# Layer 2 of a two-layer MoE: each group's outs issued inside the next group's first chain, quarters taken from PSUM

## The chip, the cores and the metric

The kernel runs on 1 core of one Trainium2 chip. The metric is the device time of one execution in microseconds (us); three runs of the kernel before gave a median of 1530.74 us (1524.88 to 1533.66). Lower is better.

## The reference

A linear attention (8 batches, 8 heads, 576 positions, width 64, normalised per position) gives 4608 tokens of width 512. They go through two feed-forward layers:

```
kv  = einsum('bhsd,bhse->bhde', k, v);  out = einsum('bhsd,bhde->bhse', q, kv)
x   = out / rms(out) * g_norm                        # 4608 x 512
h   = x @ w_in;  x2 = (h * cos(h)) @ w_out           # layer 1: 512 -> 2048 -> 512
y   = (((x2 @ w1) * (x2 @ w2)) @ w3) @ w_out2        # layer 2: 512 -> 1024 -> 1024 -> 512
```

Everything is float32.

## The kernel before

TensorE multiplies values of a rounded format (fp32r). An operand is held as a rounded half (hi, a copy by ScalarE) and a remainder (lo, a subtraction by VectorE or GpSimd); `split` (L120) issues the two. A product then takes three matmuls, hi·hi, hi·lo, lo·hi, under the lines L878, L879 and L880 for 512 columns, or a loop at L1275 for 384.

The attention and layer 1 take the first 854 us and are untouched. What follows is one program order written out by hand: each engine carries out its instructions in the order in which the code issues them.

**The wc stage (854 to 905 us).** `w3 @ w_out2` is multiplied out once, as `wc`. It has 16 steps (`emit_wc`, L1201), two halves of 8, each step 12 matmuls of 512 columns with one block of w3. A block is split two steps ahead (`split_w3`, L1175) into one of two buffers (`g_home`, L96). In between stand other pieces: the first group's right operands from x2 (`xc_steps`, L1225) on VectorE, and the first left operands from w1 and w2 (`w12_steps`, L1131) on GpSimd, in pieces named in the table `when` of the main function. At the end of each half `split_wc` splits four blocks of wc out of PSUM.

**Layer 2 (905 us to the end, `second`, L1377).** There are 12 groups: six of 768 tokens with the first half of the columns of w1 and w2 (h = 0), then the same six backwards with the second half (h = 1). A group is four chains (`Chain`). A chain is one 128-column strip of x2 @ w1 or x2 @ w2 times a 2 x 2 block scheme with 7 products, P1 to P7, each of 6 matmuls of 384 columns; its four results are the quarters q0 to q3. P1 and P2 (`open1`) make Y, which gives q0; P6 goes into X (`open2`); P5 goes into V and P7 into X (`open3`), which gives q3; P4 (`close1`) gives q2 from X, P3 (`close2`) gives q1 from V. A chain's P4 and P3 run inside the next chain, after its P2 and P6. X (two banks, "h"), V (two, "pa"), Y ("acc0", "acc1") and the outs ("acc2", "acc3") are all eight banks of PSUM.

X is read between products into a row of SBUF (`held`, L1283, ScalarE): s1 after P1, s2 after P6, s3 after P7. So P7 can't begin before s2 is taken. `done` (L1315) forms a quarter: the w1 chain of a pair keeps it in SBUF (`a`); the w2 chain adds the held row (L1334, into the row), multiplies by `a` (L1335, row by row in SBUF, or L1332 from X), and splits the product from SBUF (ScalarE L122, VectorE L124) into `ab`. The rows are 512 wide ("row", 5 buffers).

The **outs** are ab @ wc: six blocks of 128 tokens, each with two halves of 6 matmuls of 512 columns (`o_half`, L1351). Half 0 uses the first chain pair, half 1 the second; half 1 of blocks 0 to 2 needs q0 and q2 of the last chain, of blocks 3 to 5 q3 and q1. In h = 0 an out is copied (ScalarE for even blocks, L1366; VectorE for odd) and stored as a partial sum; in h = 1 VectorE adds the partial sum that was loaded back (L1372) and the result is stored. All these DMAs, and the loads of x2 (`x2r`, L1231), are issued on SP's queue.

At the end of a group the code issues: half 0 of block 0, then P4 and P3 of the fourth chain, half 0 of block 1, half 1 of blocks 0 and 1, then blocks 2 to 5. Then comes P1 of the next group.

x2 is split into 7 right operands for each group but the seventh, which has the sixth's. Its pieces are hung on places of the group before: `(k, 2, "o1")` is after `open1` of chain 2 of group k. ScalarE makes the hi halves, GpSimd the sums and the lo halves. The left operands for h = 1 are made in the sixth and seventh group.

Of the kernel before, what the change touches and what calls it, by code (L numbers as in the profile page):

```python
# [8 lines left out]
F32R = mybir.dt.float32r  # L9
# [4 lines left out]
P = 128  # L14
# [14 lines left out]
def f32(ap):  # L29
    return ap.bitcast(F32)  # L30
# [3 lines left out]
def kernel(  # L34
# [1140 lines left out]
    def split_w3(step):  # L1175
        half, c = step
        t = g_home([P, 2, 4, P], F32R, f"w3hl_{half}_{c}")
        w3[half, c] = t
        return split(t.rearrange("p i j f -> p i (j f)"), w3raw.pop(step), vec)
# [21 lines left out]
    def emit_wc(half, c):  # L1201

        t, o = w3.pop((half, c)), wo2[c]
        for j in range(4):
# [58 lines left out]
    class Chain:  # L1263
# [37 lines left out]
        def open3(self):  # L1301
            self.v = self.bank(ps_a, "pa", "V")
            self.product(5, self.v, first=True)
            self.product(7, self.x)
            self.done(3, self.v, self.held(self.x, "s3"))

        def close1(self):
            self.product(4, self.x, last=True)
            self.done(2, self.x, None)

        def close2(self):
            self.product(3, self.v, last=True)
            self.done(1, self.v, self.s2)

        def done(self, q, ps, s):  # L1315
# [26 lines left out]
            split(ab[self.h, self.g, j][:, :, H * sh:H * sh + H], s, vec)  # L1342
# [34 lines left out]
    def second():  # L1377
# [16 lines left out]

        on((0, 0, "o1"), split_wc, 1, 1)
        on((0, 0, "o2"), split_wc, 1, 2)
        on((0, 0, "o2"), split_wc, 1, 3)
        for k in range(len(order) - 1):
            if order[k + 1][1] == order[k][1]:
                continue  # L1400
            at = [(k, 1, "o3"), (k, 2, "o1"), (k, 2, "o2"), (k, 3, "o1"), (k, 3, "o2"),
                  (k, 3, "o3"), (k, 3, "end")]
            if k == NG:
                at[:3] = (k, 2, "o1"), (k, 2, "o2"), (k, 2, "o3")
            stages(lambda g=order[k + 1][1]: xc_steps(g, pool), at)
# [3 lines left out]
        def begin(dp, i):  # L1409
# [4 lines left out]
            (0, 0): ((k, 2, "c1"), (k, 2, "o3"), (k, 3, "o1"), (k, 3, "o2"), (k, 3, "o3")),  # L1414
            (0, 1): ((k, 3, "end"), (k, "o", 0), (k, "o", 1), (k, "o", 2), (k, "o", 3)),
            (1, 0): ((k, "o", 4), (k, "o", 5), (k + 1, 0, "o1"), (k + 1, 0, "o2"), (k + 1, 0, "o3")),
            (1, 1): ((k + 1, 1, "o1"), (k + 1, 1, "c1"), (k + 1, 1, "o2"), (k + 1, 1, "c2"),
                     (k + 1, 1, "o3")),
        }
        for key, at in places.items():  # L1420
# [4 lines left out]
        n = 0  # L1425
        for k, (h, g) in enumerate(order):
            prev = None
            for at in range(4):
                c = Chain(h, g, *divmod(at, 2))
# [17 lines left out]
            o_half(h, g, 0, 0)  # L1447
            prev.close1()
            prev.close2()
            do(k, 3, "end")  # L1450
            o_half(h, g, 1, 0)
            for s in range(GT // P):
                if s > 1:
                    o_half(h, g, s, 0)
                o_half(h, g, s, 1)
                do(k, "o", s)
# [136 lines left out]
    if True:  # L1593
# [24 lines left out]
        with tc.manual_schedule(  # L1618
# [24 lines left out]
            for i, ks in enumerate(((0, 1, 2, 3, 3), (4, 5, 6, 7, 7), (8, 9, 10, 11, 13),  # L1643
                                    (12, 13, 14, 15, 15))):
                for k in ks:
                    when.setdefault(k, []).append(sets[i])
            when.setdefault(2, []).append(sets[2])
            when.setdefault(4, []).append(sets[3])
            for k in (5, 6, 7, 12, 13, 14):
                when.setdefault(k, []).append(x0)  # L1650
            for k, step in enumerate(wc_steps):
# [3 lines left out]
                if k + 2 < len(wc_steps):  # L1655
                    split_w3(wc_steps[k + 2])
# [4 lines left out]
            split_wc(1, 0)  # L1661
            second()
# [59 lines left out]
```

## Time and profile before

| what | value |
|---|---|
| median of 3 runs | 1530.74 us |
| the profiled execution's own time | 1533.62 us |
| its span in the trace | 1531.8 us |
| TensorE's mean granted clock in it | 0.988 |
| TensorE, matmuls | 1458.9 us, 95% |
| VectorE | 960.1 us, 63% |
| ScalarE | 696.1 us, 45% |
| GpSimd | 649.0 us, 42% |
| first P1 of the 12 groups | 905.15 us |
| last add of an out | 1527.66 us |

The share of busy time counts overlapping matmuls by their modelled ends, so it is no measure of what could be saved; the waits of one engine and the length of a stage are. The first matmul of P1 starts, for the 12 groups, at 905.15, 965.86, 1017.05, 1068.25, 1119.46, 1170.67, 1216.53, 1275.56, 1326.72, 1379.46, 1430.65 and 1481.81 us. Each group holds the same 240 matmuls, so the distances can be compared with each other.

### The profile page before, as it was taken

What the parts mean: (1) busy time and instruction counts of PE and PEld (TensorE: products, weight loads), DVE (VectorE), ACT (ScalarE), POOL (GpSimd) and SP (SyncE); (2) the same over time, 40 slices, a digit from 0 to 9 for tenths busy, and PEclk for the clock granted to TensorE, in tenths of its full rate; (3) what the DMA queues carried; (4) which work ended last, traced back from release to release, by engine and by line L of the source; (5) the groups of instructions that cost most, each with busy time, mean ns of one, the idle gap of its engine ahead of it and who ended that gap; (6) DMA issues with size and microseconds to landing.
All of it is one profiled execution on the core that took longest, in us unless ns stands there. A gap on an engine that the chain in (4) does not pass through costs nothing.

```text
span 1531.8 us, 21181 instructions
## 1 busy us (share of the span) xinstructions
PE 1458.9 (95%) x7632; PEld 1240.0 (81%) x7632; DVE 960.1 (63%) x1408; ACT 696.1 (45%) x1328; POOL 649.0 (42%) x504
## 2 busy tenths in 40 slices
PE   8999999999999999999999978998899979889988
PEld 6877777787778889888888767987898969778878
DVE  4797575574879667898888555444544354455444
ACT  4666565555556455555555443323332442233221
POOL 0174664575554622221224465325522672355230
PEclk8999999999999999999999989999999999999999
DMA  8366986797589989999999710221122123312321
GB/s 315 119 209 185 325 266 202 243 316 242 198 302 346 362 296 316 344 333 355 336 357 357 258 42 15 69 83 50 46 70 96 42 76 117 124 43 82 124 83 56
DMA packets 146506, 298.75 MB, mean 195 GB/s; under 512 B 16256, under 2 KB 54240, under 8 KB 146400
## 3 DMA queue, kind: packets, MB, share of 16 engines
q1 hardware_dynamic: 145696, 296.80, 56.3%
q8 instruction: 60, 0.98, 0.3%
q10 hardware_dynamic: 704, 0.59, 0.1%
q14 instruction: 46, 0.38, 0.1%
HBM read 184.92 MB, written 112.42 MB: 194 GB/s over the span
## 4 chain that ended last, share of the span: by engine, by line
PE 72%; DVE 15%; ACT 5%; issue 3%; DMA 2%; POOL 2%; SPq 1%; ACTq 0%; DVEq 0%; POOLq 0%
PE X L1052 13%; PE X L1275 8%; PE h L878 7%; PE h L879 7%; PE h L880 7%; PE V L1052 6%; DVE s L1335 4%; PE o L878 3%; PE Y L1052 3%; PE o L879 3%; PE o L880 3%; DVE ab L124 3%; PE V L1275 3%; PE Y L1275 2%; ACT ab L122 2%
## 5 line engine op out<-in xcount | busy, mean ns | idle before, releaser
L124 POOL TENSOR_TENSOR xc<-x2r,xc 128x768 fp32r<-128x768 f32 x70 | 134.1, 1934 | 267.3 <-ACT xc L122 249.7
L1275 PE MATMUL X<-xc,w 128*128 128x384 f32 x1152 | 221.9, 337 | 17.8 <-ACT s L1283 17.8
L878 PE MATMUL h<-x,w_in 128*128 128x512 f32 x576 | 234.2, 407 | 4.0 <-DVE u L1520 3.8
L879 PE MATMUL h<-x,w_in 128*128 128x512 f32 x576 | 224.8, 390 | 0.2 <-DVE x L124 0.2
L880 PE MATMUL h<-x,w_in 128*128 128x512 f32 x576 | 225.0, 391 | 0.0
L1275 PEld LDWEIGHTS X<-xc,w 128*128 128x128 f32 x1152 | 202.2, 188 | 23.6 <-ACT s L1283 21.6
L1052 PE MATMUL X<-g_hl,wl 128*128 128x512 f32 (+1 forms) x960 | 199.7, 368 | 0.0
L1052 PEld LDWEIGHTS X<-g_hl,wl 128*128 128x128 f32 x960 | 167.3, 189 | 30.2 <-DVE wl L124 0.2
L124 POOL TENSOR_TENSOR g_hl<-g_raw,g_hl 128x1024 fp32r<-128x1024 f32 x29 | 73.6, 2537 | 232.3 <-ACT g_hl L122 168.1
L124 DVE TENSOR_TENSOR g_hl<-g_raw,g_hl 128x1024 fp32r<-128x1024 f32 x97 | 140.3, 1473 | 39.9 <-ACT g_hl L122 39.8
L1546 DVE SCALAR_TENSOR_TENSOR u<-h,r 128x512 f32<-128x512 f32 x136 | 93.5, 688 | 109.7 <-ACT r L1545 89.6
L122 ACT ACTIVATE g_hl<-g_raw 128x1024 fp32r<-128x1024 f32 x126 | 130.4, 1057 | 52.3 <-DMA g_raw<-g 42.8
L1283 ACT ACTIVATE s<-X 128x384 f32<-128x384 f32 x144 | 68.9, 486 | 173.1 <-PE X L1275 173.0
L878 PE MATMUL o<-wchl,ab 128*128 128x512 f32 x288 | 117.5, 408 | 27.8 <-DVE part L1372 10.9
L1545 ACT ACTIVATE r<-h 128x512 int32<-128x512 f32 x136 | 81.3, 597 | 131.0 <-PE h L880 130.5
L878 PEld LDWEIGHTS h<-x,w_in 128*128 128x128 f32 x576 | 108.1, 188 | 35.8 <-DVE u L1520 9.1
L880 PEld LDWEIGHTS h<-x,w_in 128*128 128x128 f32 x576 | 108.1, 188 | 23.3
L879 PEld LDWEIGHTS h<-x,w_in 128*128 128x128 f32 x576 | 108.3, 188 | 22.9 <-DVE x L124 0.7
L880 PE MATMUL o<-wchl,ab 128*128 128x512 f32 x288 | 115.9, 403 | 3.5 <-DVE ab L124 3.5
L879 PE MATMUL o<-wchl,ab 128*128 128x512 f32 x288 | 114.9, 399 | 0.0
L122 ACT ACTIVATE ab<-s 128x384 fp32r<-128x384 f32 x72 | 37.8, 525 | 163.2 <-DVE s L1335 163.2
L1275 PE MATMUL V<-xc,w 128*128 128x384 f32 x576 | 109.6, 334 | 0.0
(164 smaller groups left out, 2608.0 us busy)
## 6 DMA issues: line engine op xcount, KB each, us to landing
g_raw<-g SPq DMA_DIRECT2D x126, 512.0 KB
x2r<-x_all SPq DMA_DIRECT2D x44, 384.0 KB
kvraw<-in_kv_main_dram SPq DMA_DIRECT2D x32, 512.0 KB
g<-ta SPq DMA_DIRECT2D x32, 512.0 KB
g<-tb SPq DMA_DIRECT2D x32, 512.0 KB
g<-u SPq DMA_DIRECT2D x28, 512.0 KB
g<-u SPq DMA_DIRECT2D x40, 256.0 KB
part<-o SPq DMA_DIRECT2D x36, 256.0 KB
```

The source lines that it names most:

```text
L122: hi = nc.scalar.activation(dst[:, 0], src, AF.Copy)
L124: lo = lo_engine.tensor_tensor(dst[:, 1], src, f32(dst[:, 0]), ALU.subtract)
L878: nc.tensor.matmul(ps, w[0], x[0], start=first, stop=False)
L879: nc.tensor.matmul(ps, w[0], x[1], start=False, stop=False)
L880: return nc.tensor.matmul(ps, w[1], x[0], start=False, stop=last).ins
L1052: nc.tensor.matmul(ps, w[:, a, i2, ws], g[:, b, q], start=first and half == 0 and q == 0 and n == 0, stop=last and final and q == KH - 1 a ...
L1275: nc.tensor.matmul(ps, w[:, self.i, a, k], x[:, b, k], start=first and k == 0 and n == 0, stop=last and k == 1 and n == 2, skip_group_chec ...
L1283: nc.scalar.activation(s, ps, AF.Copy)
L1335: vec.tensor_tensor(s, s, a, ALU.mult)
L1545: nc.scalar.activation(r, h_ps[n], AF.Identity, bias=0.25, scale=INV_2PI)
L1546: nc.vector.scalar_tensor_tensor(u, h_ps[n], INV_2PI, r, ALU.mult, ALU.subtract)
```

## The change

There are four parts.

1. **The outs' place** (`second`). A group's outs no longer stand behind its fourth chain but inside the first chain of the next group (`edge`): P1, P2, then P4 of the old chain, half 0 of blocks 0 and 1, P6, half 1 of block 0, P3 of the old chain, half 1 of block 1 and both of block 2, P5, P7, then blocks 3 to 5. Only the twelfth group's outs stand behind it.
2. **Values in PSUM** (`done`). The sum and the product of a quarter are written to PSUM (`to`: Y for q0 and q3, X for q2, V for q1), and the split reads them there. The first chain's Y lies in a "pa" bank.
3. **w3's blocks** lie in a ring of four buffers (two `g_home`, two pairs of rows), and are split three steps ahead instead of two.
4. **Places**: the pieces of x2's operands and of the w1, w2 sets hang on other places; five pieces of the last set of h = 0 go into the first group, and the split of wc's block (1, 0) stands after the first `open1`.

```
     def split_w3(step):
         half, c = step
-        t = g_home([P, 2, 4, P], F32R, f"w3hl_{half}_{c}")
+        if c % 4 < 2:
+            t = g_home([P, 2, TB], F32R, f"w3hl_{half}_{c}")
+            t = t[:, 0], t[:, 1]
+        else:
+            t = tuple(row(f"w3hl_{half}_{c}_{i}").bitcast(F32R) for i in range(2))
...
-            y = self.bank(ps_acc, f"acc{n % 2}", "Y")
-            self.product(2, y, first=True, last=True)
-            self.done(0, y, s)
+            self.y = self.bank(*((ps_acc, f"acc{n % 2}") if n else (ps_a, "pa")), "Y")
+            self.product(2, self.y, first=True, last=True)
+            self.done(0, self.y, s, self.y)
...
-            self.done(3, self.v, self.held(self.x, "s3"))
+            self.done(3, self.v, self.held(self.x, "s3"), self.y)
...
-            self.done(2, self.x, None)
+            self.done(2, self.x, None, self.x)
...
-            self.done(1, self.v, self.s2)
+            self.done(1, self.v, self.s2, self.v)
...
-            if s is None:
-                s = row(f"ab_{self.name}")[:, 0:H]
-                vec.tensor_tensor(s, ps, a, ALU.mult)
-            else:
-                vec.tensor_tensor(s, ps, s, ADD)
-                vec.tensor_tensor(s, s, a, ALU.mult)
+            if s is not None:
+                vec.tensor_tensor(to, ps, s, ADD)
+                ps = to
+            vec.tensor_tensor(to, ps, a, ALU.mult)
...
-            split(ab[self.h, self.g, j][:, :, H * sh:H * sh + H], s, vec)
+            split(ab[self.h, self.g, j][:, :, H * sh:H * sh + H], to, vec)
...
-            at = [(k, 1, "o3"), (k, 2, "o1"), (k, 2, "o2"), (k, 3, "o1"), (k, 3, "o2"),
-                  (k, 3, "o3"), (k, 3, "end")]
+            at = [(k, 1, "o3"), (k, 2, "o2"), (k, 2, "o3"), (k, 3, "o2"), (k, 3, "o3"),
+                  (k + 1, 0, "c1"), (k + 1, 0, "o2")]
...
+                edge = k > 0 and at == 0
                 c = Chain(h, g, *divmod(at, 2))
                 c.open1(n)
...
+                if edge:
+                    outs(k - 1, (0, 0), (1, 0))
                 c.open2()
                 do(k, at, "o2")
+                if edge:
+                    outs(k - 1, (0, 1))
                 if prev:
                     prev.close2()
                 do(k, at, "c2")
+                if edge:
+                    outs(k - 1, (1, 1), (2, 0), (2, 1))
                 c.open3()
                 do(k, at, "o3")
+                if edge:
+                    outs(k - 1, *both[6:])
...
-                if k + 2 < len(wc_steps):
-                    split_w3(wc_steps[k + 2])
+                if k + 3 < len(wc_steps):
+                    split_w3(wc_steps[k + 3])
...
-            split_wc(1, 0)
-            second()
+            second(sets[3])
```

The order of TensorE at the end of the fourth group and the start of the fifth, in the kernel before. A name's number tells one buffer's use from another; X_10080 and V_10134 are the fourth chain's, X_10279 the next group's first chain's, o_10160 and o_10190 the outs of blocks 0 and 1.

```order
L1275 MATMUL X_10080<-xc_5_9776,w_01_5_8644 128x384 x6
L878 MATMUL o_10160<-wchl_8551,ab_9961 128x512
...
L1275 MATMUL X_10080<-xc_6_9809,w_01_2_8605 128x384 x6
L1275 MATMUL V_10134<-xc_2_9779,w_01_6_8707 128x384 x6
L878 MATMUL o_10190<-wchl_8551,ab_9961 128x512
...
L878 MATMUL o_10160<-wchl_8557,ab_10098 128x512
...
L1275 MATMUL X_10279<-xc_0_10030,w_00_0_8381 128x384 x6
L1275 MATMUL Y_10288<-xc_1_10101,w_00_1_8384 128x384 x6
```

The same place after the change: X_10081 and V_10131 are the fourth chain's, X_10155 and Y_10164 the next group's.

```order
L1282 MATMUL X_10081<-xc_5_9806,w_01_5_8685 128x384 x6
L1282 MATMUL X_10155<-xc_0_10049,w_00_0_8386 128x384 x6
L1282 MATMUL Y_10164<-xc_1_10118,w_00_1_8389 128x384 x6
L1282 MATMUL X_10081<-xc_6_9834,w_01_2_8628 128x384 x6
L878 MATMUL o_10188<-wchl_8553,ab_9963 128x512
...
L878 MATMUL o_10195<-wchl_8553,ab_9963 128x512
...
L1282 MATMUL X_10155<-xc_4_10121,w_00_4_8467 128x384 x6
L878 MATMUL o_10188<-wchl_8559,ab_10099 128x512
...
L1282 MATMUL V_10131<-xc_2_9809,w_01_6_8742 128x384 x6
L878 MATMUL o_10195<-wchl_8559,ab_10099 128x512
```

P1 and P2 of the next group now stand ahead of the old chain's P4, and 12 out matmuls and P6 stand between P4 and the first out that reads the last chain's quarters (ab_10099).

ScalarE's order in the fourth chain of the same group, before: the first row is s1, s_0311_10121 is s2, s_0311_10147 is s3, xc_1 and xc_4 are hi halves of the next group's right operands.

```order
L1283 ACTIVATE s_0311_10087<-X_10080 128x384
L122 ACTIVATE ab_10098<-s_0311_10087 128x384
L122 ACTIVATE xc_1_10101<-x2r_10007 128x768
L122 ACTIVATE xc_4_10104<-x2r_10007 128x768
L1325 ACTIVATE a_1_10113<-X_10012 128x384
L1283 ACTIVATE s_0311_10121<-X_10080 128x384
L122 ACTIVATE xc_3_10123<-x2r_10007 128x768
L1283 ACTIVATE s_0311_10147<-X_10080 128x384
```

And after:

```order
L1290 ACTIVATE s_0311_10088<-X_10081 128x384
L122 ACTIVATE ab_10099<-Y_10090 128x384
L1332 ACTIVATE a_1_10108<-X_10014 128x384
L1290 ACTIVATE s_0311_10116<-X_10081 128x384
L122 ACTIVATE xc_1_10118<-x2r_10009 128x768
L122 ACTIVATE xc_4_10121<-x2r_10009 128x768
L1290 ACTIVATE s_0311_10144<-X_10081 128x384
L122 ACTIVATE ab_10148<-Y_10090 128x384
```

s2 moved ahead of the two right operands, which now follow P6 of the fourth chain, and the quarter is rounded from Y.

VectorE's order in the second half of the wc stage, before: w3hl is the lo half of a block of w3 (its number in the half stands behind it), wchl a block of the first half of wc, xc and x2r the first group's right operands.

```order
L124 TENSOR_TENSOR w3hl_0_8529<-w3raw_8423,w3hl_0_8529 128x512
L1245 TENSOR_TENSOR x2r_8302<-x2r_8302 128x768
L1246 TENSOR_TENSOR x2r_8302<-x2r_8302 128x768
L124 TENSOR_TENSOR wchl_8551<-wc_0_8357,wchl_8551 128x512
...
L124 TENSOR_TENSOR wchl_8560<-wc_3_8369,wchl_8560 128x512
L124 TENSOR_TENSOR w3hl_1_8564<-w3raw_8423,w3hl_1_8564 128x512
L124 TENSOR_TENSOR xc_1_8572<-x2r_8302,xc_1_8572 128x768
```

And after:

```order
L1185 TENSOR_TENSOR w3hl_1_8534<-w3raw_8428,w3hl_1_8534 128x512
L1252 TENSOR_TENSOR x2r_8302<-x2r_8302 128x768
L1253 TENSOR_TENSOR x2r_8302<-x2r_8302 128x768
L124 TENSOR_TENSOR wchl_8553<-wc_0_8361,wchl_8553 128x512
...
L124 TENSOR_TENSOR wchl_8562<-wc_3_8373,wchl_8562 128x512
L1185 TENSOR_TENSOR w3hl_2_1_8567<-w3raw_8482,w3hl_2_0_8566 128x512
L124 TENSOR_TENSOR xc_1_8575<-x2r_8302,xc_1_8575 128x768
```

Behind the four blocks of wc there now stands the third block of w3, not the second.

## Rows read from the trace of the kernel before

**Rows 1.** The page's busy time of each engine (share of the span, instructions).
```profile
PE 1458.9 (95%) x7632; PEld 1240.0 (81%) x7632; DVE 960.1 (63%) x1408; ACT 696.1 (45%) x1328; POOL 649.0 (42%) x504
```
**Rows 2.** Waits of TensorE: line <- releaser: us in total, times, longest us.
```profile
PE X L1275 <- ACT s L1283: 17.8, 12, 2.1
PE o L878 <- DVE part L1372: 10.9, 5, 2.9
PE o L878 <- ACT o L1366: 10.0, 5, 2.0
PE o L878 <- ACT ab L122: 7.0, 10, 0.7
PE Y L1275 <- DVE wchl L124: 5.7, 1, 5.7
...
PE o L880 <- DVE ab L124: 3.5, 10, 0.4
```
**Rows 3.** Windows: us, busy (x) of PE, PEld, DVE, ACT, POOL, PEclk, DMA, GB/s.
```profile
854.45:905.15 50.70, 46.93 (x193) 36.68 (x192) 31.09 (x33) 25.70 (x53) 36.84 (x38) 0.97 0.39 130
905.15:965.86 60.71, 50.58 (x241) 45.42 (x240) 28.56 (x37) 20.86 (x40) 28.10 (x18) 0.92 0.14 48
965.86:1017.05 51.19, 46.74 (x241) 42.40 (x240) 24.07 (x31) 17.03 (x32) 21.64 (x11) 1.00 0.18 62
...
1170.67:1216.53 45.86, 45.83 (x241) 42.59 (x240) 17.66 (x31) 17.78 (x42) 18.14 (x25) 1.00 0.22 80
1216.53:1275.56 59.03, 50.15 (x242) 44.44 (x240) 26.71 (x34) 19.24 (x40) 36.45 (x31) 0.94 0.24 81
...
1481.81:1531.80 49.99, 45.82 (x241) 42.40 (x239) 20.02 (x35) 10.60 (x22) 0.00 (x0) 0.99 0.21 69
```
**Rows 4.** TensorE's timeline, second group's end: start, us, instruction, [idle before <- releaser].
```profile
993.49 1.32 PE L1275 MATMUL X<-xc,w 128*128 128x384 f32 x6 [1.44 <-ACT s L1283]
...
996.05 1.21 PE L1275 MATMUL X<-xc,w 128*128 128x384 f32 x6
997.09 1.20 PE L1275 MATMUL V<-xc,w 128*128 128x384 f32 x6
...
1001.06 0.51 PE L878 MATMUL o<-wchl,ab 128*128 128x512 f32 x1 [0.69 <-ACT ab L122]
...
1006.03 0.50 PE L878 MATMUL o<-wchl,ab 128*128 128x512 f32 x1 [1.98 <-ACT o L1366]
```
**Rows 5.** VectorE, layer 2, by shape: xcount | busy us, mean ns | idle
```profile
L1335 DVE TENSOR_TENSOR s<-s,a 128x384 f32<-128x384 f32 x72 | 79.2, 1101 | 2.5
L124 DVE TENSOR_TENSOR ab<-s,ab 128x384 fp32r<-128x384 f32 x72 | 61.9, 859 | 44.1 <-ACT ab L122 44.1
...
L1334 DVE TENSOR_TENSOR s<-V,s 128x384 f32<-128x384 f32 x48 | 26.5, 553 | 64.5 <-ACT s L1283 63.8 <-PE V L1275 0.7
```
**Rows 6.** VectorE's product line alone: ns min/median/max, first and last start.
```profile
L1335 DVE TENSOR_TENSOR s<-s,a x72: 557/1146/1895, 921.2 to 1514.1; 128x384 f32<-128x384 f32 x72
```
**Rows 7.** VectorE by shape up to 905 us: a write into PSUM.
```profile
L961 DVE TENSOR_TENSOR w_ps<-w_out,w_ps 128x512 f32<-128x512 f32 x4 | 2.8, 688 | 0.0
```
**Rows 8.** ScalarE, from the page's groups: the rounded half of a quarter.
```profile
L122 ACT ACTIVATE ab<-s 128x384 fp32r<-128x384 f32 x72 | 37.8, 525 | 163.2 <-DVE s L1335 163.2
```
**Rows 9.** GpSimd's timeline, second group: x2's first operand to its fourth sum.
```profile
982.05 1.84 POOL L124 TENSOR_TENSOR xc<-x2r,xc 128x768 fp32r<-128x768 f32 x1 [27.46 <-ACT xc L122]
...
988.08 2.16 POOL L1246 TENSOR_TENSOR x2r<-x2r 128x768 f32<-128x768 f32 x1
```
**Rows 10.** TensorE's timeline in the wc stage.
```profile
884.79 0.50 PE L880 MATMUL wc<-wo,w3hl 128*128 128x512 f32 x1 [1.90 <-DVE w3hl L124]
```
**Rows 11.** VectorE's timeline in the wc stage.
```profile
883.73 1.00 DVE L124 TENSOR_TENSOR w3hl<-w3raw,w3hl 128x512 fp32r<-128x512 f32 x1
```
**Rows 12.** Windows: five us after that wait.
```profile
885.00:890.00 5.00, 5.00 (x16) 3.92 (x16) 3.65 (x4) 2.49 (x6) 3.93 (x5) 0.66 0.01 2
```
**Rows 13.** Chain of waits, seventh group: start us, us, what.
```profile
1235.86 3.57 DMA x2r<-x_all
```

More of the change, by code (lines that the diff above doesn't have):

```diff
@@ L1176, in split_w3 @@
         half, c = step
-        t = g_home([P, 2, 4, P], F32R, f"w3hl_{half}_{c}")
+        if c % 4 < 2:
[3 more added lines that the diff above has]
+            t = tuple(row(f"w3hl_{half}_{c}_{i}").bitcast(F32R) for i in range(2))
         w3[half, c] = t
-        return split(t.rearrange("p i j f -> p i (j f)"), w3raw.pop(step), vec)
+        raw = w3raw.pop(step)
+        nc.scalar.activation(t[0], raw, AF.Copy)
+        vec.tensor_tensor(t[1], raw, f32(t[0]), SUB)
     def wc_tile(j, name):
@@ L1203, in emit_wc @@
         t, o = w3.pop((half, c)), wo2[c]
+        t = [w.rearrange("p (j f) -> p j f", j=4) for w in t]
         for j in range(4):
@@ L1211, in emit_wc @@
             three(
-                acc[j], (t[:, 0, j], t[:, 1, j]), (o[:, 0], o[:, 1]), c == 0, c == NJ - 1
+                acc[j], (t[0][:, j], t[1][:, j]), (o[:, 0], o[:, 1]), c == 0, c == NJ - 1
             )
@@ L1304, in open3, with done @@
             self.product(7, self.x)
-            self.done(3, self.v, self.held(self.x, "s3"))
+            self.done(3, self.v, self.held(self.x, "s3"), self.y)
         def close1(self):
             self.product(4, self.x, last=True)
-            self.done(2, self.x, None)
+            self.done(2, self.x, None, self.x)
         def close2(self):
             self.product(3, self.v, last=True)
-            self.done(1, self.v, self.s2)
-        def done(self, q, ps, s):
+            self.done(1, self.v, self.s2, self.v)
+        def done(self, q, ps, s, to):
             key = (self.h, self.g, self.dp)
@@ L1375, in o_half, with second @@
             load_part(g, s + 4)
-    def second():
+    def second(last_set):
         order = [(0, g) for g in range(NG)] + [(1, g) for g in reversed(range(NG))]
@@ L1393, in stages @@
                 on(key, lambda: next(made[0], None))
+        on((0, 0, "o1"), split_wc, 1, 0)
         on((0, 0, "o1"), split_wc, 1, 1)
@@ L1413, in second @@
         places = {
[L1414 to L1418, printed above, removed]
-        }
+            (0, 0): ((k, 2, "c1"), (k, 2, "o2"), (k, 2, "o3"), (k, 3, "o1"), (k, 3, "c1")),
+            (0, 1): ((k, 3, "o2"), (k, 3, "o3"), (k + 1, 0, "o1"), (k + 1, 0, "c1"),
+                     (k + 1, 0, "o2")),
+            (1, 0): ((k, "o", 0), (k, "o", 1), (k, "o", 2), (k + 1, 0, "o3"), (k, "o", 3)),
+            (1, 1): ((k, "o", 4), (k, "o", 5), (k + 1, 1, "o1"), (k + 1, 1, "c1"),
+                     (k + 1, 1, "o2")),
+        }
+        for place in ((0, "o2"), (0, "o3"), (1, "o2"), (1, "o3"), (2, "o2")):
+            on((0, *place), lambda: next(last_set, None))
         for key, at in places.items():
@@ L1423, in second, with outs @@
                 on(place, lambda key=key: next(sets[key], None))
-        n = 0
+        n, prev = 0, None
+        def outs(k, *parts):
+            for s, half in parts:
+                o_half(*order[k], s, half)
+                if half == 1:
+                    do(k, "o", s)
+        both = [(s, half) for s in range(GT // P) for half in range(2)]
         for k, (h, g) in enumerate(order):
-            prev = None
             for at in range(4):
+                edge = k > 0 and at == 0
                 c = Chain(h, g, *divmod(at, 2))
@@ L1446, in second @@
                 prev = c
[L1447 to L1456, printed above, removed]
+        outs(k, (0, 0))
+        prev.close1()
+        outs(k, (1, 0))
+        prev.close2()
+        outs(k, (0, 1), (1, 1), *both[4:])
         assert not todo
@@ L1642 @@
             when = {}
-            for i, ks in enumerate(((0, 1, 2, 3, 3), (4, 5, 6, 7, 7), (8, 9, 10, 11, 13),
-                                    (12, 13, 14, 15, 15))):
+            for i, ks in enumerate(((0, 1, 2, 3, 4), (5, 6, 7, 8, 10), (2, 9, 11, 12, 13, 15), (5,))):
                 for k in ks:
                     when.setdefault(k, []).append(sets[i])
-            when.setdefault(2, []).append(sets[2])
-            when.setdefault(4, []).append(sets[3])
+            split_w3(wc_steps[2])
             for k in (5, 6, 7, 12, 13, 14):
```

2 lines of the change are left out of this document (removed).

## The prediction

> **What bounds the kernel now.** I read the busy times first: TensorE is occupied 95% of the span and no other engine over 63% [rows 1], so what counts is what TensorE waits for and how long its stages last. The list of its waits comes next [rows 2]. Six lines make 54.9 us together: 17.8 us before a product into X, until ScalarE has copied X; 10.9 and 10.0 us before an out, until VectorE or ScalarE has emptied the bank of an earlier out; 7.0 and 3.5 us before an out, until the last quarter is rounded and its remainder taken; 5.7 us once, for a block of wc. All belong to layer 2, and all but the last stand at a group's end.
>
> Then I cut layer 2 at the first P1 of each group [rows 3]. All groups have the same 240 matmuls. A usual one takes 51.19 us. The sixth, in which no right operands of x2 are made, takes 45.86 with TensorE busy for 45.83: that is a group without waits, measured. The first takes 60.71 and the seventh 59.03, at a granted clock of 0.92 and 0.94. TensorE's timeline at a usual end [rows 4] shows where 5.3 us go: 1.44 before P7 (s2 behind other copies on ScalarE), 0.69 for the last quarter, 0.35 for its remainder (the 3.5 us of the list over ten ends) and 1.98 for a bank that ScalarE empties late, 4.5 in all; the rest is in slower matmuls right behind such waits.
>
> What makes the quarters late is VectorE: the product in rows of SBUF takes 1101 ns on the mean and the remainder 859, while a sum that reads one operand from PSUM takes 553 [rows 5]; the shortest product took 557, the longest 1895 [rows 6]. The stretch has to do with where operands lie.
>
> **Part 1, the outs inside the next first chain.** It adds no instruction. The unit is a product of 6 matmuls, 1.04 us from start to start [rows 4]; 28 of them are 29.1 of the 45.86 us, so the 12 out halves take (45.86 - 29.1)/12 = 1.39 each. With the next group's P1 at 0: P4 of the old chain ends at 3.1, half 0 of blocks 0 and 1 at 5.9, P6 at 6.9. Half 1 of block 0 reads q2 from its fourth matmul on, at about 7.6. q2 is one product on VectorE (0.55), a copy on ScalarE (0.53, [rows 8]) and a remainder (0.55 to 0.86) behind 3.1: ready by 5.1, at latest about 6 with one copy ahead of it. So the waits for ScalarE's and VectorE's last quarter go (7.0 + 3.5). Block 0's bank is emptied by about 9.1, needed for block 2 at 10.8; block 1's by 12.4, needed for block 3 at 15.6. So the waits for outs' banks go (10.0 + 10.9). P7 of the old chain needs s2, which now stands ahead of xc_1 and xc_4 on ScalarE: copied about 1.3 before P7 is due (17.8). What comes late next, if anything, is below.
>
> A P4 that waited would hold up everything behind it on TensorE's queue. It needs s3, copied by 0.7; P4 begins at 2.1.
>
> **Part 2, values in PSUM.** Per quarter of a w2 chain nothing is added or removed, only moved: sum, product and remainder read one operand from PSUM each. The sum that does so takes 553 [rows 5]; a write into PSUM by VectorE, 512 wide, took 688 ns [rows 7], which is 516 for 384. I take 0.55 each. Bounded from the other side by today's 1.10 and 0.86, q2 would still be ready before 7.6. So the length of VectorE's work is not what the gain hangs on: the order hides it. X, V and Y stay occupied for about 2 us longer; the next user of each bank comes a chain (7.3 us) later or more, so this costs nothing, and would cost up to 2 us per chain only if a chain's banks turned over in less than that.
>
> The Trainium skill, page "SBUF — State Buffer", section "Who interferes with whom", gives a reason: a VectorE instruction with two SBUF inputs contends with a GpSimd instruction that reads SBUF, one with at most one does not. The rows of VectorE agree (553 against 1101). By that rule GpSimd's operands would also come earlier at the edges, and the sum below would be up to 2.5 us less.
>
> **Part 4, places.** New on the path: xc_1's remainder. GpSimd can begin once ScalarE has rounded xc_0, behind s2 of the third chain, whose P6 ends 10.4 before the next P1. From there: two ScalarE copies (0.5, and 0.8 for twice the width), xc_0's remainder to the end of the sum for t2 and b12 8.19 us, xc_1's remainder 1.84 [rows 9], 0.3 of handing over: 11.7. It is read by P2's second matmul at 1.2, so there is room for 11.6. I charge 0.25 at each of ten edges, 2.5 together; 0.8 more at the first (a piece of the last w set stands between on GpSimd); 0.7 in the sixth group, where copies of w pieces stand ahead of s2. Bounds: nothing, and the longest wait of TensorE on such a copy, 2.1 [rows 2], at each edge.
>
> The loads of x2 are issued on SP behind the six stores of the outs, now about 24 after P1. One load took 3.57 us to land [rows 13]; first use is at about 36, so some 6 us are spare.
>
> **Sum for layer 2.** From the first P1 (905.15) to the twelfth (1481.81) are 576.66 us for eleven groups [rows 3]; eleven at 45.86 are 504.5, so -72.2. The twelfth has no wait today either, and keeps its own outs. New waits +4.0. Of the 72.2, the first group gives 14.9, and there the gain past the usual 5.3 needs that the wait of 5.7 for wc [rows 2] goes: the first Y lies in a "pa" bank now and waits for no block of wc. Left over, this costs up to 9.5 with the clock that falls behind it.
>
> **Part 3, w3's ring.** The wc stage takes 50.70 us [rows 3]; 192 matmuls at 0.227 (the rate where none waits; 43.5) leave 7.2. The largest wait, 1.90, ends with VectorE's remainder of a w3 block at 884.7 [rows 10, 11]; the granted clock is 0.66 on the mean in the five us behind it [rows 12], so TensorE ran most of them at the lower of its two levels (1.2 instead of 2.4 GHz) after it had stood still, which loses 0.34 x 5 = 1.7. The same instruction on VectorE now makes the block of one step later. VectorE is full there, so its time stays near 884.7; TensorE without the waits ahead of it reaches that step's third matmul, the 123rd, at 854.45 + 122 x 0.227 = 882.1 and waits 2.7; I take 0.8 more at the next step, whose block stands behind two remainders of xc on VectorE; with the same fall of the clock 5.2 are lost instead of 7.2: -2.0. Bounds: 0 and -7.2.
>
> **Total.** -72.2 + 4.0 - 2.0 = -70.2. The profiled span of 1531.8 becomes 1461.6, its own time of 1533.62 about 1463.4. It lies 2.9 above the median of the runs, 1530.74, from which 1460.5 follows. I forecast 1462.
>
> **The rivals.** (B) *GpSimd's chain becomes the bound at each edge.* For: it has only 0.1 us too little room by my sum, and a delay of any of five operations adds up there. Against: it stood at 42% [rows 1], and before nothing of TensorE waited for it. Each edge then costs up to 2.1 of wait [rows 2] and 1.7 for a clock that falls behind it, as after the wait in the wc stage [rows 12], 3.8 in place of 0.25: ten edges 35.5, 1497.5. Still faster.
>
> (C) *The slower side: x2's loads come late.* They are issued behind six stores on one queue, and each store must wait for an out that now ends 23 us into the next group. If a load landed later than about 6 us past my time the whole chain of right operands would shift, and TensorE would stand at P2 of the next group for the excess. Ten edges at 7 us eat the 70: it decides from a landing of some 16 us instead of 3.57. Against: the DMA engines are at 0.18 in a usual group [rows 3]. Beyond 16 us slower, say 1550; between, about the same as before.
>
> (D) *Values in PSUM stay stretched, or the order alone gives all.* Bounded in part 2: no other time than the forecast's, for another reason. I hold that for 0.1 of the forecast's chance.
>
> **How the numbers follow.** The forecast 0.74 (D's 0.1 in it), within its own range of 1449 to 1475; B 0.18; C 0.08, half of it slower and half about equal. The low end: no new wait, and a wc stage without waits, 1460.5 - 4.0 - 5.2 = 1451, with outs at 1.36 a little less, 1449. The high end is B's. So 1449 to 1498. Less than 0.5% (about 7.5 us) can't be told from no change; faster 0.92, same 0.04, slower 0.04.
>
> **What would show it.** In the changed kernel's waits of TensorE, the lines for ScalarE's copy of X, the outs' banks and the last quarter should be gone or under 0.5 us each, and the distances from P1 to P1 should be 46 to 46.5 in all groups. VectorE's product and remainder should be near 550 ns. If I am right on GpSimd, a wait of 0.1 to 0.4 before Y on xc stands at the edges, at B some 2 with a clock near 0.66; at C, SP's stores and x2r stand ahead of it in the chain of waits. A wait of about 2.7 on a w3 block in the wc stage shows part 3. It would be wrong if P4 or the first outs in the edge wait for quarters, or if X or V come free late.

## The result, and the profile after

The changed kernel takes 1454.77 us (median of 4 runs, 1452.64 to 1458.59), the kernel before beside it 1528.26: a ratio of 0.952 with a 95% interval of 0.948 to 0.956. The forecast was 1462, with 1449 to 1498 as its range. The profiled execution took 1458.59 us, its span 1456.7. The page's busy times, against [rows 1]:

```profile
PE 1437.9 (99%) x7632; PEld 1236.0 (85%) x7632; DVE 896.4 (62%) x1408; ACT 695.5 (48%) x1328; POOL 633.0 (43%) x504
```

The list of what TensorE waits for, as in [rows 2], here with the lines that belong to the wc stage and layer 2 (us in total, times, longest):

```profile
PE wc L880 <- DVE w3hl L1185: 2.5, 2, 1.5
PE X L1282 <- ACT s L1290: 1.0, 1, 1.0
...
PE o L878 <- DVE part L1377: 0.2, 1, 0.2
```

All six lines of [rows 2] are gone but for one wait on s2 and one on an out. The windows that answer to [rows 3] (length, busy and count of PE, PEld, DVE, ACT, POOL, granted clock, DMA share, GB/s): the wc stage, first P1 to second, a usual group, the seventh.

```profile
855.75:902.33 46.58, 44.11 (x194) 35.89 (x192) 36.20 (x35) 23.83 (x48) 36.33 (x33) 1.00 0.40 142
902.33:929.57 27.24, 27.24 (x157) 26.99 (x156) 13.61 (x24) 14.53 (x32) 15.91 (x16) 1.00 0.18 58
929.57:975.25 45.68, 45.68 (x242) 42.68 (x241) 17.42 (x31) 17.08 (x32) 20.63 (x12) 1.00 0.20 70
...
1157.95:1204.93 46.98, 45.97 (x242) 42.69 (x241) 17.33 (x31) 20.26 (x46) 30.79 (x36) 1.00 0.25 91
```

A usual group has TensorE busy from end to end, 45.68 us instead of 51.19. The first stretch is short because the first group's outs and its last chain's P4 and P3 lie in the next one. The clock is at 1.00 everywhere. In the kernel before it was lower in the wc stage and in the first, the seventh and the ninth group, with 0.97, 0.92, 0.94 and 0.97 on the mean ([rows 3], the ninth from its own window); 50.70 x 0.03 + 60.71 x 0.08 + 59.03 x 0.06 + 52.74 x 0.03 make an estimated 11 to 12 us, which the lower clock cost in these four stretches. VectorE's groups (xcount | busy us, mean ns | idle before), which answer to [rows 5]: the product, the remainder.

```profile
L1340 DVE TENSOR_TENSOR Y<-Y,a 128x384 f32<-128x384 f32 x48 | 27.2, 566 | 1.6
L124 DVE TENSOR_TENSOR ab<-Y,ab 128x384 fp32r<-128x384 f32 x48 | 26.8, 558 | 27.1 <-ACT ab L122 27.1
```

1101 and 859 ns have become 566 and 558. In short: from the first P1 to the end of the span 554.37 us instead of 626.65, 72.3 less; the wc stage 4.1 less; the stages ahead of it, which the change doesn't touch, 1.3 more. That is 75.1 between the two spans.

**How runs are compared below.** The first wc matmul, behind 850 us of the same code, began between 850.1 and 858.7 us in the profiles of these kernels. So beside the whole time, the stretch from there to the end of the span is given: 677.4 us before, 601.0 after. The wc stage is in it: with the same code there it took between 45.8 and 46.6 us in the changed kernel and in experiments 1, 3, 7, 8 and 11, so a difference of less than a microsecond in this stretch shows nothing by itself.

### The profile page after: what moved, and what is told of

Its sections match the earlier page's. It is cut to its first block, busy times and chain, and to the rows that moved or that the text cites. A ratio compares the mean times of both kernels' runs of the same rounds, so it can differ in the third digit from the quotient of the medians.

```text
span 1456.7 us, 21195 instructions
## 1 busy us (share of the span) xinstructions
PE 1437.9 (99%) x7632; PEld 1236.0 (85%) x7632; DVE 896.4 (62%) x1408; ACT 695.5 (48%) x1328; POOL 633.0 (43%) x504
## 4 chain that ended last, share of the span: by engine, by line
PE 88%; DVE 6%; DMA 2%; issue 1%; ACT 1%; SPq 1%; POOL 0%; DVEq 0%; ACTq 0%
PE X L1282 14%; PE X L1052 13%; PE h L878 7%; PE h L879 7%; PE h L880 7%; PE V L1282 7%; PE V L1052 6%; PE o L880 4%; PE o L879 4%; PE o L878 4%; PE Y L1282 3%; PE Y L1052 3%; PE kv L285 2%; PE out L686 1%; DMA g<-u 1%
## 5 line engine op out<-in xcount | busy, mean ns | idle before, releaser
L124 POOL TENSOR_TENSOR xc<-x2r,xc 128x768 fp32r<-128x768 f32 x70 | 128.1, 1851 | 213.1 <-ACT xc L122 212.7
L880 PE MATMUL o<-wchl,ab 128*128 128x512 f32 x288 | 113.0, 392 | 0.0
L879 PE MATMUL o<-wchl,ab 128*128 128x512 f32 x288 | 112.8, 392 | 0.0
L878 PE MATMUL o<-wchl,ab 128*128 128x512 f32 x288 | 112.1, 389 | 0.2 <-DVE part L1377 0.2
L1282 PEld LDWEIGHTS V<-xc,w 128*128 128x128 f32 x576 | 101.2, 188 | 1.9
```

What stands on the lines that cost most here:

```text
L124: lo = lo_engine.tensor_tensor(dst[:, 1], src, f32(dst[:, 0]), ALU.subtract)
L878: nc.tensor.matmul(ps, w[0], x[0], start=first, stop=False)
L879: nc.tensor.matmul(ps, w[0], x[1], start=False, stop=False)
L880: return nc.tensor.matmul(ps, w[1], x[0], start=False, stop=last).ins
L1282: nc.tensor.matmul(ps, w[:, self.i, a, k], x[:, b, k], start=first and k == 0 and n == 0, stop=last and k == 1 and n == 2, skip_group_chec ...
```

## The experiments

**1. The values back in SBUF.**

```
-            if s is not None:
-                vec.tensor_tensor(to, ps, s, ADD)
-                ps = to
-            vec.tensor_tensor(to, ps, a, ALU.mult)
+            if s is None:
+                s = row(f"ab_{self.name}")[:, 0:H]
+                vec.tensor_tensor(s, ps, a, ALU.mult)
+            else:
+                vec.tensor_tensor(s, ps, s, ADD)
+                vec.tensor_tensor(s, s, a, ALU.mult)
...
```

> The changed kernel with part 2 undone: sums and products of the quarters are again written to rows of SBUF and split from there; the order, the ring and the places stay as changed. Theory (the order hides VectorE's stretch): the product is again near 1.1 us and the remainder 0.86 to 1.05, GpSimd's sums 2.04 instead of 1.85; q2 comes about 1.8 us later than in the changed kernel, just as its first reader is due, and xc_1's remainder some 0.2 late, so a usual group takes 45.7 to 46.7 us instead of 45.68 and the time is 1 to 8 us above the changed kernel's 1454.8 (1456 to 1463). Rival (the values in PSUM carry the gain): the waits for the quarter and for the outs' banks, 3 us a group, come back: 48.7 us a group, 1485 or more.

Measured: 1463.62 us, 0.959 of before (0.955 to 0.962); 608.1 us from the first wc matmul, 7.2 above the changed kernel. A usual group:

```profile
1066.03:1112.33 46.30, 46.18 (x241) 42.64 (x241) 23.72 (x32) 17.02 (x33) 22.06 (x12) 1.00 0.20 69
```

The theory holds; the time is 0.6 us above the expected range. VectorE's product and remainder are stretched again, to 0.97 and 1.10 us on the mean. GpSimd's sum for b12, the last one ahead of xc_1's remainder (ns, min/median/max), goes from 1849/1854/1862 in the changed kernel to 2139/2156/2168 here, and P2 of the next group lasts 1.60 us on TensorE's timeline instead of 1.20, because xc_1's remainder comes in the middle of it:

```profile
1067.08 1.60 PE L1282 MATMUL Y<-xc,w 128*128 128x384 f32 x6
```

**2. The values in PSUM alone**, on the kernel before.

```
...
+            if s is not None:
+                vec.tensor_tensor(to, ps, s, ADD)
+                ps = to
+            vec.tensor_tensor(to, ps, a, ALU.mult)
...
-            split(ab[self.h, self.g, j][:, :, H * sh:H * sh + H], s, vec)
+            split(ab[self.h, self.g, j][:, :, H * sh:H * sh + H], to, vec)
```

> The kernel before with part 2 alone: values in PSUM, everything else as before. Theory (two ways to the same waits): product and remainder fall to 0.55, so at a usual end the wait for the quarter (0.69 + 0.35) goes, that for ScalarE's out (1.98) and for s2 (1.44) fall by about half: 48 to 49.5 us a group instead of 51.19, the time 1493 to 1512 instead of 1528. Rival 1 (only the order matters): groups stay at 51, 1523 to 1530. Rival 2 (the values carry all): groups near 46, 1465.

Measured: 1472.78 us, 0.965 (0.962 to 0.967); 617.8 us from the first wc matmul, 59.6 of the 76.4 us less than before. Of these, 1.5 lie in the wc stage, which this edit leaves as it was (see 4), and 58.1 behind the first P1. The theory was wrong, rival 2 nearly right: a usual group has no wait left.

```profile
1053.48:1099.48 46.00, 46.00 (x242) 42.55 (x241) 17.43 (x31) 16.91 (x32) 20.05 (x11) 1.00 0.20 69
...
1191.22:1242.72 51.50, 46.70 (x242) 42.51 (x241) 19.41 (x34) 18.99 (x40) 34.09 (x31) 1.00 0.28 93
```

I had taken off a half from each wait. But VectorE's sums, products and remainders stand one behind the other at a group's end, and the products and remainders all got shorter, so the whole delay went. The timelines at a usual end show it for s2: ScalarE begins to copy it 4.7 us after the fourth chain's P2 begins. P2 and the copy, here:

```profile
1028.29 1.20 PE L1275 MATMUL Y<-xc,w 128*128 128x384 f32 x6
1033.02 0.49 ACT L1283 ACTIVATE s<-X 128x384 f32<-128x384 f32 x1
```

and in the kernel before, in the group of [rows 4], 6.3 us:

```profile
986.68 1.20 PE L1275 MATMUL Y<-xc,w 128*128 128x384 f32 x6
992.95 0.48 ACT L1283 ACTIVATE s<-X 128x384 f32<-128x384 f32 x1
```

What the values alone leave is the seventh group (51.50), the first, and the wc stage.

**3. x2's pieces at the old places**, all else changed.

```
-            at = [(k, 1, "o3"), (k, 2, "o2"), (k, 2, "o3"), (k, 3, "o2"), (k, 3, "o3"),
-                  (k + 1, 0, "c1"), (k + 1, 0, "o2")]
+            at = [(k, 1, "o3"), (k, 2, "o1"), (k, 2, "o2"), (k, 3, "o1"), (k, 3, "o2"),
+                  (k, 3, "o3"), (k + 1, 0, "c1")]
+            if k == NG:
+                at[:3] = (k, 2, "o1"), (k, 2, "o2"), (k, 2, "o3")
```

> The changed kernel with x2's pieces at the places of before (the last one after P4 in the next group's first chain). Theory: s2 of the fourth chain is again taken behind the two right operands on ScalarE, so P7 waits 0.8 to 1.4 us at ten ends, 46.5 to 47.1 us a group, 1463 to 1470. Rival (with the quarter's product short, ScalarE comes to these copies early enough): no wait over 0.3 us, within 3 us of 1454.8.

Measured: 1460.17 us, 0.956 (0.955 to 0.958); 602.4 us from the first wc matmul, 1.5 above. The rival holds: 45.88 us a group, no wait at P7.

**4. w3's blocks in two buffers.**

```
-        if c % 4 < 2:
-            t = g_home([P, 2, TB], F32R, f"w3hl_{half}_{c}")
-            t = t[:, 0], t[:, 1]
-        else:
-            t = tuple(row(f"w3hl_{half}_{c}_{i}").bitcast(F32R) for i in range(2))
+        t = g_home([P, 2, TB], F32R, f"w3hl_{half}_{c}")
+        t = t[:, 0], t[:, 1]
...
-                if k + 3 < len(wc_steps):
-                    split_w3(wc_steps[k + 3])
+                if k + 2 < len(wc_steps):
+                    split_w3(wc_steps[k + 2])
```

> The changed kernel with w3's blocks in two buffers and split two steps ahead, as before; the new table of pieces in the wc stage stays. Theory (the ring gives the stage its gain): the wc stage takes 49 to 50.7 us instead of 46.55, the rest is the same, 1457 to 1459. Rival (the new places of the w pieces give it): 46.5 to 47.5 us.

Measured: 1460.13 us, 0.956 (0.955 to 0.958); the wc stage (the window's length first) takes 2.75 us more than in the changed kernel:

```profile
854.03:903.36 49.33, 45.09 (x194) 35.67 (x193) 32.42 (x34) 25.48 (x50) 31.80 (x33) 1.00 0.38 134
```

So of the stage's 4.1 us the ring gives 2.75. The other 1.4, nearly, is the clock's, which was at 0.97 in the profile of the kernel before. Experiments 2 and 9 have the stage as it was before, and with the clock at 1.00 they took 49.17 and 49.46 us in it, as long as here. Experiment 2:

```profile
858.73:907.90 49.17, 45.09 (x194) 35.56 (x192) 32.02 (x34) 25.45 (x52) 36.63 (x37) 1.00 0.39 134
```

The new places of the w pieces give this stage nothing that can be seen.

**5. and 6. The first group.** The first Y's bank and the split of wc's block (1, 0) as before (5), and the w pieces of the wc stage at their old places (6).

```
-            self.y = self.bank(*((ps_acc, f"acc{n % 2}") if n else (ps_a, "pa")), "Y")
+            self.y = self.bank(ps_acc, f"acc{n % 2}", "Y")
...
-        on((0, 0, "o1"), split_wc, 1, 0)
...
+            split_wc(1, 0)
             second(sets[3])
```

```
-            for i, ks in enumerate(((0, 1, 2, 3, 4), (5, 6, 7, 8, 10), (2, 9, 11, 12, 13, 15), (5,))):
+            for i, ks in enumerate(((0, 1, 2, 3, 3), (4, 5, 6, 7, 7), (8, 9, 10, 11, 13),
+                                    (12, 13, 14, 15, 15))):
...
+            when.setdefault(2, []).append(sets[2])
+            when.setdefault(4, []).append(sets[3])
```

> The changed kernel with the very first Y back in bank acc0 and wc's block (1, 0) split ahead of the first P1, as before; all else as changed. Theory of the prediction (the bank is what freed the first group): P2 waits 5 to 6 us for VectorE's remainder of that block and the clock falls behind it, so from the first P1 to the second 34 to 37 us instead of 27.24. Rival (the wait came from ScalarE, which stood behind w pieces that waited for GpSimd, and those pieces are now elsewhere): P2 waits 1 us at most, 27.2 to 28.5.

> The changed kernel with the w pieces of the wc stage at the places of before (the last set is finished in that stage); the first Y stays in a pa bank. Theory of the prediction (the bank): first group 27.2 to 28 us. Rival (ScalarE's queue): s1 and s2 of the first chains stand behind w copies that wait for GpSimd until some 5 us after the first P1, so products into X wait 3 to 6 us: 31 to 37.

Measured, one execution each: 1458.62 and 1459.35 us; 600.8 and 607.4 us from the first wc matmul. The stretches from the first P1 to the second, of 5:

```profile
902.37:929.64 27.27, 27.27 (x157) 27.02 (x156) 13.03 (x23) 14.05 (x31) 15.95 (x16) 1.00 0.18 58
```

and of 6, with five us behind its wait:

```profile
896.29:930.44 34.15, 30.08 (x157) 29.76 (x156) 15.80 (x26) 14.80 (x30) 15.27 (x13) 0.90 0.14 47
...
902.62:907.62 5.00, 5.00 (x16) 5.00 (x17) 3.05 (x5) 2.39 (x5) 0.48 (x1) 0.50 0.72 265
```

With the new places the bank is worth nothing; the places are worth 6.9 us. ScalarE's timeline in 6 (the idle time before, and what ended it, in brackets) shows the way: the first P1's s1 stands behind w copies that wait for GpSimd.

```profile
900.97 0.42 ACT L122 ACTIVATE w<-w12raw 128x256 fp32r<-128x256 f32 x1 [1.62 <-POOL w12raw L1154]
901.77 0.42 ACT L122 ACTIVATE w<-w12raw 128x256 fp32r<-128x256 f32 x1 [0.39 <-POOL w12raw L1156]
902.10 0.47 ACT L1290 ACTIVATE s<-X 128x384 f32<-128x384 f32 x1
```

The next product into X waits 4.07 us for it, and the clock then goes down to its lower level (0.50).

**7. GpSimd's chain later.**

```
-            at = [(k, 1, "o3"), (k, 2, "o2"), (k, 2, "o3"), (k, 3, "o2"), (k, 3, "o3"),
+            at = [(k, 1, "o3"), (k, 2, "o3"), (k, 2, "o3"), (k, 3, "o2"), (k, 3, "o3"),
```

> The changed kernel with xc_0's pieces one place later (after P7 of the third chain instead of P6), so that GpSimd's chain begins 2.1 us later. Theory: in the changed kernel xc_1's remainder is ready 0.7 us before P2 reads it, so P2 now waits 1.2 to 1.5 us at each of ten edges: 46.9 to 47.2 us a usual group, the time 12 to 16 us above the changed kernel. Rival (the prediction's case B): the clock falls behind each such wait, 48.5 us or more a group, 30 us or more in all. Third: GpSimd's operations have slack elsewhere, no wait.

Measured: 1482.39 us, one execution; 628.3 us from the first wc matmul, 27.4 above. TensorE waits at all ten edges, 2.2 us at the longest. The line of its waits:

```profile
PE Y L1282 <- POOL xc L124: 21.5, 10, 2.2
```

The third group, behind whose wait the clock fell, and the fourth, where it did not:

```profile
973.96:1023.64 49.68, 47.53 (x242) 43.96 (x241) 17.54 (x31) 17.09 (x33) 19.95 (x12) 0.97 0.19 64
1023.64:1071.77 48.13, 45.98 (x242) 42.70 (x241) 17.53 (x31) 17.09 (x33) 19.95 (x12) 1.00 0.19 66
```

The wait is longer than expected because I miscounted: three products lie between the two places (P3 of the chain before, P5, P7), 3.1 us, not two. 3.1 less 0.75 of room gives 2.3. The clock fell behind two of the ten waits, the second and the tenth. The five us from the end of the tenth wait:

```profile
1411.07:1416.07 5.00, 5.00 (x18) 4.47 (x19) 1.68 (x3) 2.01 (x5) 5.00 (x3) 0.66 0.00 0
```

So the price of B was right in its wait and wrong in its clock.

**8. The new order, values in SBUF and x2's pieces at the old places** (the edits of 1 and 3 together).

> The changed kernel with part 2 undone (values in rows of SBUF) and x2's pieces at the places of before: the new order of outs with the ring is what is left. Theory (without short values the places count: s2 of the fourth chain stands behind a late quarter and two right operands on ScalarE): P7 waits 1.2 to 1.6 at ten ends, 47.3 to 48 us a group, 1473 to 1485. Rival (the order hides everything, whatever the places): 46.3 us a group as with the new places, 1460 to 1466.

Measured: 1487.72 us, 0.973 (0.970 to 0.976); 630.5 us from the first wc matmul. A usual group takes 48.72, over the expected range, as is the whole time, with two waits, 1.44 for s2 and a second one that I had not expected, on the last quarter's remainder. From TensorE's timeline:

```profile
1076.86 2.37 PE L1282 MATMUL X<-xc,w 128*128 128x384 f32 x12 [1.44 <-ACT s L1290]
...
1087.34 0.50 PE L880 MATMUL o<-wchl,ab 128*128 128x512 f32 x1 [1.04 <-DVE ab L124]
```

VectorE's remainder that it waits for is q2's, stretched to 2.00 us:

```profile
1085.29 2.00 DVE L124 TENSOR_TENSOR ab<-ab,ab 128x384 fp32r<-128x384 f32 x1 [0.59 <-ACT ab L122]
```

**9. and 10. What stretches VectorE**, on the kernel before: the product read from PSUM and written to SBUF (9), and read from SBUF and written to PSUM (10).

```
...
+            if s is not None:
+                vec.tensor_tensor(to, ps, s, ADD)
+                ps = to
+            to = row(f"ab_{self.name}_{q}")[:, 0:H]
+            vec.tensor_tensor(to, ps, a, ALU.mult)
...
```

```
...
+            if s is not None:
+                vec.tensor_tensor(s, ps, s, ADD)
+                ps = s
+            vec.tensor_tensor(to, ps, a, ALU.mult)
...
```

> The kernel before with a quarter's sum written to PSUM and the product read from there, but the product written to a row of SBUF and the remainder taken from that row. Theory (two operands from SBUF stretch VectorE beside GpSimd, wherever the result goes): product 0.55 to 0.57, remainder 0.86 to 1.1 us, GpSimd's sums between 1.85 and 2.04; a usual group 46.5 to 49 us. Rival (writing into SBUF is what stretches): the product stays near 1.1.

> The kernel before with a quarter's sum in a row of SBUF and the product read from there, but written into PSUM, and the remainder taken from PSUM. Theory (two operands from SBUF): product near 1.1 us, remainder 0.55; a usual group 48 to 50.5 us. Rival (the place of the result): product 0.55.

Measured, one execution each: 1476.63 and 1520.11 us; 46.6 us a usual group in 9. In 10 two usual groups take 48.3 us, as expected, and six take 51.6, over the range. Two neighbours in 10:

```profile
964.72:1013.01 48.29, 46.50 (x241) 42.40 (x240) 20.72 (x31) 16.69 (x32) 20.89 (x11) 1.00 0.19 66
1013.01:1064.61 51.60, 48.09 (x242) 43.56 (x241) 22.47 (x31) 16.69 (x32) 20.54 (x11) 0.97 0.18 62
```

In the longer ones the wait for an out's bank is 2.6 us instead of 0.9, and the clock falls behind it. VectorE's groups of 9, the remainder, which at 733 ns is shorter than expected, and the product:

```profile
L124 DVE TENSOR_TENSOR ab<-ab,ab 128x384 fp32r<-128x384 f32 x96 | 70.4, 733 | 59.0 <-ACT ab L122 59.0
L1334 DVE TENSOR_TENSOR ab<-Y,a 128x384 f32<-128x384 f32 x48 | 26.8, 557 | 1.6
```

and of 10, the product for q0 and q3, for q1, and the remainder:

```profile
L1333 DVE TENSOR_TENSOR Y<-s,a 128x384 f32<-128x384 f32 x48 | 50.3, 1048 | 1.7
L1333 DVE TENSOR_TENSOR V<-s,a 128x384 f32<-128x384 f32 x24 | 37.3, 1556 | 0.8
...
L124 DVE TENSOR_TENSOR ab<-Y,ab 128x384 fp32r<-128x384 f32 x48 | 26.8, 558 | 27.0 <-ACT ab L122 27.0
```

It is the operands: with two from SBUF an instruction is stretched, with one it takes 0.56 us, wherever the result goes. And it is stretched only beside GpSimd. In the kernel before, all 31 products with two SBUF operands that ran while GpSimd ran nothing took 557 to 560 ns; of the 41 others 40 took longer, 1511 on the mean of the 41. In its twelfth group, where GpSimd is idle ([rows 3]), the products are (ns, min/median/max, first and last start):

```profile
L1335 DVE TENSOR_TENSOR s<-s,a x6: 557/558/560, 1490.0 to 1514.1; 128x384 f32<-128x384 f32 x6
```

**11. All but the order.** The changed kernel with the loop of `second` as before.

```
-                if edge:
-                    outs(k - 1, (0, 0), (1, 0))
...
+            o_half(h, g, 0, 0)
+            prev.close1()
+            prev.close2()
+            do(k, 3, "end")
+            o_half(h, g, 1, 0)
...
```

> The changed kernel with the outs back at the end of their own group: part 1 undone, the rest as changed. Theory (with the values in PSUM the old order waits for nothing at a group's end): 45.9 to 46.2 us a usual group instead of 45.68, 3 to 6 us above the changed kernel. Rival (the order carries a part of its own): waits for quarters or banks of 1 us and more come back, 47 us or more.

Measured: 1463.12 us, 0.956 (0.952 to 0.959); 607.5 us from the first wc matmul, 6.5 above: 46.24 us a usual group and 48.08 the seventh. A little over what was expected: 0.2 of it is a wait for GpSimd's xc.

**12. Fewer waits.** The two places where the changed kernel still waits.

```
-            for k in (5, 6, 7, 12, 13, 14):
+            for k in (5, 9, 11, 12, 13, 14):
...
-            (1, 1): ((k, "o", 4), (k, "o", 5), (k + 1, 1, "o1"), (k + 1, 1, "c1"),
-                     (k + 1, 1, "o2")),
+            (1, 1): ((k, "o", 4), (k, "o", 5), (k + 1, 1, "o1"), (k + 1, 1, "o2"),
+                     (k + 1, 1, "o3")),
```

> The changed kernel with two tables altered: the first group's x2 pieces on VectorE at steps 5, 9, 11, 12, 13, 14 of the wc stage instead of 5, 6, 7, 12, 13, 14, and two w pieces of the seventh group one or two products later. Theory: the waits for w3's remainder (1.51 and 0.95) shrink to under 1 us together, since two sums of x2 no longer stand ahead of the split on VectorE, and the wait of 1.01 for s2 in the seventh group goes: 2.5 to 3.5 us less from the first wc matmul to the end (600.95 in the changed kernel), the ratio to the changed kernel 0.998. Rival: the pieces moved later stand before the first group's operands, and P5 or P7 of the first chain waits instead; no gain.

Measured: 1451.24 us, 0.949 of before (0.946 to 0.951); 598.1 us from the first wc matmul, 2.8 less. The wc stage and the eighth group:

```profile
850.09:893.63 43.54, 43.54 (x194) 36.05 (x193) 34.10 (x34) 23.66 (x48) 35.28 (x33) 1.00 0.43 151
1195.07:1242.09 47.02, 45.96 (x241) 42.68 (x241) 19.62 (x34) 15.47 (x29) 21.92 (x13) 1.00 0.29 101
```

The wc stage waits for nothing now, and takes 3.0 us less than in the profile of the changed kernel, 2.2 less than the shortest of the others with its code. The wait in the seventh group went, and one of 1.06 us for GpSimd's xc took its place an edge later. In the whole times the two intervals overlap, so the gain is shown for the wc stage, not for the kernel's time.

## Why the prediction was right

The usual group in us, from the first P1 to the next, by what was changed:

| outs' order | values | x2's places | us |
|---|---|---|---|
| old | SBUF | old | 51.19 (before) |
| old | PSUM | old | 46.00 (2) |
| old | PSUM | new | 46.24 (11) |
| new | SBUF | old | 48.72 (8) |
| new | SBUF | new | 46.30 (1) |
| new | PSUM | old | 45.88 (3) |
| new | PSUM | new | 45.68 (after) |

**The sum held.** A group without waits was taken at 45.86; it is 45.68. From the first P1 on, 72.3 us went where 68.2 were forecast. The profiled span fell by 75.1, the forecast said 70.2. That the total held where a reason did not, in the first group above all, is luck.

**The reason was half of it.** "So the length of VectorE's work is not what the gain hangs on: the order hides it" is right in that the new order with long values (1) needs 46.30 us. But it needs x2's new places for that: without them (8) it is 48.72, and there q2's remainder is 1.04 us late, which my bound ("still ready before 7.6") excluded. The bound took the mean of 0.86 us for a remainder that took 2.00, and left out that q2 stands behind q3's remainder and a sum on VectorE. And short values need no new order at all (2). The two parts are two ways to the same waits; their gains, 5.2 by one, 2.5 by the other with the old places, don't add up. On the changed kernel the order is worth 6.5 us, on top of everything else. D, to which I gave 0.1 within the forecast, asked whether the order alone gives all: with the new places it gives most, and the values give most without it.

**Part 1's copies.** P7's wait for s2 did go, and for that s2 need not stand ahead of xc_1 and xc_4, as I wrote: at the old places (3) the wait is gone as well, with the quarter that ScalarE rounds ahead of it coming early. With long values the places do it (1); with neither (8) P7 waits 1.44 us.

**The new waits were mis-sized.** Of +4.0 us 1.0 came, in the seventh group, not the sixth. Before, two of the twelve waits for s (1.69 and 1.11 us) stood in the seventh group's first chain as well, and not at a group's end, where I put them all. GpSimd's chain was charged 0.25 at each edge (its terms add up to 11.63, not 11.7, against 11.6 of room), with 8.19 us from xc_0's remainder to b12. In the changed kernel the same four instructions stand at

```profile
1057.78 1.85 POOL L124 TENSOR_TENSOR xc<-x2r,xc 128x768 fp32r<-128x768 f32 x1 [24.52 <-ACT xc L122]
...
1063.44 1.85 POOL L1253 TENSOR_TENSOR x2r<-x2r 128x768 f32<-128x768 f32 x1
```

which is 7.51 us: xc_1's remainder is done at about 1067.1, and P2's second matmul is due at 1067.8. With the values in SBUF (1) it is late by about what I said. So part 2 shortened GpSimd's work too, and the sum left that out. I had drawn this consequence in one sentence from the Trainium skill ("SBUF — State Buffer", "Who interferes with whom"); 9 and 10 agree with its rule on two SBUF inputs.

**The first group: right size, wrong cause.** I put its gain past the usual on the bank of the first Y. Experiment 5 shows 0.03 us for that, experiment 6 shows 6.9 for the w pieces, which stood ahead of ScalarE's copies. So this part, up to 9.5 us of the sum, was luck: it came because part 4 moved the w pieces. The row named VectorE's remainder of wc as the one that came last; what made that late was ScalarE's queue, whose copies of w waited for GpSimd. The last such copy but one, the copy of wc and its remainder, in the kernel before:

```profile
909.56 0.42 ACT L122 ACTIVATE w<-w12raw 128x256 fp32r<-128x256 f32 x1 [2.32 <-POOL w12raw L1154]
...
910.69 0.58 ACT L122 ACTIVATE wchl<-wc 128x512 fp32r<-128x512 f32 x1
...
911.30 0.69 DVE L124 TENSOR_TENSOR wchl<-wc,wchl 128x512 fp32r<-128x512 f32 x1 [3.03 <-ACT wchl L122]
```

**The wc stage was undersized:** 4.1 for 2.0. The floor of 43.5 was right: without waits the stage took 43.54 (12). TensorE waited 1.51 and 0.95 instead of 2.7 and 0.8, since VectorE reached that block a microsecond earlier in the stage. And the clock, which I let fall as in [rows 12], stayed at 1.00, which is about 1.4 of the 4.1. That fall did not come in 2 and 9 either, which have the old stage, so this share hangs on the profile compared with and not on the change alone.

**The rivals.** B's wait did not come, and C's load did not either: the DMAs behind the stores had ended by about 1098.2 us in the fifth group, ScalarE's first use began at 1102.5, so about 4 us were spare, where 6 were reckoned.

## What to carry to other kernels

Two changes that remove the same wait are not worth the sum of their gains: try each alone before crediting either. Where VectorE runs beside GpSimd, count for each of its instructions how many operands come from SBUF; moving one of them to PSUM shortened both engines' work here without a line of scheduling. A wait that names an engine is answered by reading that engine's queue back to where it stood idle, and here that led past VectorE, which the list named, to ScalarE and from there to GpSimd.

## What was not expected of the hardware

The same wait of 1.90 us (1.91 in 10) for w3's remainder stands in the wc stage of the kernel before and of experiments 2, 9 and 10, which are alike up to there. In the five us behind it the granted clock was 0.66 in before and in 10, and 1.00 in 2 and 9. After a wait of 3.08 in experiment 4 it was 1.00. Of the ten waits of 2.15 in experiment 7 two brought a fall, of the waits of 2.6 in 10 all seven (the first group has one too), and the wait of 5.7 to 5.8 for wc did so in all four kernels that have it (before, 2, 9 and 10). What decides whether TensorE goes to its lower level (1.2 GHz) is not the length of the wait just before alone, and these runs leave it open. A fall cost 1.5 to 1.7 us (49.68 against 48.13 in experiment 7; 0.34 of 5 us in [rows 12]; 51.60 less 48.29 less 1.7 of longer wait in 10), and 2.8 in 6, behind the wait of 4.07 (34.15 less 27.24 less 4.07): as much as a wait itself.
